# Attention, mixture of experts and gated layer in one kernel: attention steps in pairs, later weight splits, last k tile last

## The chip, the cores and the metric

The kernel runs on one core of a Trainium2 chip, in one launch. The metric is the device time of an execution in microseconds. PE is the matrix engine (TensorE), DVE the vector engine, ACT the scalar engine, POOL the GpSimd engine, SP the engine whose queue issues nearly all DMAs here. PE, DVE, ACT and POOL each work through their own instructions in program order, and they wait for one another through semaphores.

## The reference

For `q`, `k`, `v` of 2 x 8 x 576 x 64 two attentions are added. The coarse one averages four neighbouring positions of each and attends over the 144 that are left; the local one attends over the positions less than 4 away.

```python
q_d = q.reshape(B, H, Sd, factor, D).mean(axis=3)      # k_d and v_d likewise
out_d = sm_attn(q_d, k_d, v_d)
out_up = np.repeat(out_d, factor, axis=2)
mask = np.abs(pos[:, None] - pos[None, :]) < factor
...
return (out_up + out_local).astype(np.float32)
```

The result is `x`, 1152 tokens x 512. It goes through eight experts, `out += P[:, e] * (relu(x @ w1[e]) @ w2[e])` with 1024 hidden columns each, where `P` is a balanced gating of `x @ w_gate`. Then comes `(a * b) @ w_out` with `a = x @ w_a`, `b = x @ w_b`. All is float32.

## The kernel before, in words

**Precision.** A matrix is kept as a high part of type fp32r and the rest, a low part. A product is three matmuls: high by high, low by high, high by low. Splitting one weight block (128 x 512) is an ACT cast (L134) and a DVE subtraction (L135). A block lies in a ring of 13 slots, and three more lie in spare space. A weight load brings 256 KB into one of two staging buffers (tile `raw`, L409), and each buffer holds two blocks.

**Stages.** The experts are worked in units of half an expert. Tokens come in three blocks of 384 (`b` in the loop at L1297). In blocks 0 and 1 only the first two units (`n`, both halves of expert 0) are worked, while the attention of the later tokens is still running. For each unit there are four groups (`g_plain`, L446: 128 hidden columns by 384 tokens, four k tiles of 128, three matmuls each), whose result is a high and a low part of the hidden values. After the eight groups come six output tiles (`o_moe`, L488: 128 tokens by 512, twelve matmuls). After every group and every output tile `step()` (L1282) is called. In block 2 the same begins, the attention is over, the softmax of the gating runs beside it, and from there on products are combined in a way that saves one in eight. That part is some 85% of the time and isn't touched.

**Attention.** It is a generator, `side()` (L1103). There are 24 items (a third of a batch entry's positions, two heads), worked in a software pipeline of 29 iterations `s`. Each iteration is cut by `yield` into two half steps. The first half has, on PE, the transposes of q and k (a1) and the scores of the item before (b1); around them ACT copies and scales (a2, c3, d3), DVE maxima, sums and reductions (b4, b2, a3), and POOL the softmax's product and the low part `xl` of the result (L964, L1030). The second half has the products with v (d1) and the transposes of the probabilities (c1) on PE, on ACT the factor of the coarse output (d2a, L1010) and the exponentials (b3), on DVE d2 and c2, and on POOL the sums of four values (`sum_vd`, L865 and L868). Head pair 3, which fills k tile 3, comes last. When 384 tokens are complete, two more half steps make their gating logits (`logits`, L1039). In all 64 half steps do work, and the 65th call closes the attention (`close_attention`, L1231), which frees its buffers.

In a3 (L906), for the items that start a head pair (`u == 0`, eight of the 24), DVE sums four keys (L909) and multiplies the 128 x 144 result by 1/16 (L912, tile `kd`). The scores of the coarse attention (L931) use it one half step later.

**Order of the work.** It is fixed when the program is written. Before block 0 the loop at L1298 runs 23 half steps with nothing else; after each, `warm(3)` puts three dummy matmuls (tile `wz`, L1169; 16 stand at the very start) on PE, and after half steps 14, 16, 18, 20 and 22 one weight block is split. Then `step()` after a group splits one more block and adds 1.25 to a counter that pays for half steps, so that most groups are followed by one half step and each fourth by two. Ahead of the output tiles of block 0 the loop at L1315 splits what is missing of the 16 blocks. Before block 1 a half step is run if the tokens aren't complete (one is), and before block 2 what is left of the attention runs bare (six calls). `load_some` (L220) issues at most one weight load in each half step, and takes a staging buffer again two half steps after its second split.

**PSUM.** Groups and output tiles take turns in two banks (`bank("g")`), the attention in six.

Of the kernel before, what the change touches and what calls it, by code (L numbers as in the profile page):

```python
# [19 lines left out]
def attn_moe_glu_kernel(  # L20
# [16 lines left out]
    nc = tc.nc  # L37
# [6 lines left out]
    KT = DM // 128  # L44
    NT = N // 128
    NB = 3
    TB = N // NB
# [11 lines left out]
    def mm(o, l, r, start, stop, check=True):  # L59
        nc.tensor.matmul(out=o, lhsT=l, rhs=r, start=start, stop=stop, skip_group_check=not check)  # L60
# [11 lines left out]
    def bank(kind):  # L72
        if ps3 is not None and kind == "g":
            pool, tag = ps3, "g3"
        else:
            pool, tag = ps1, "g1"
        return pool.tile([128, 512], F32, tag=tag, name=tag)
# [6 lines left out]
    xh = xp.tile([128, KT, N], F32R, name="xh")  # L84
    xl = xp.tile([128, KT, N], F32R, name="xl")
# [6 lines left out]
    M = Model()  # L92
# [319 lines left out]
    units = []  # L412
    for e in range(E):
        for hf in range(2):
            u = Unit()
# [7 lines left out]
    for g in range(GU):  # L423
        u = Unit()
# [18 lines left out]

    GP = [[gp.tile([128, 4, TB], F32R, tag=f"{x}{n}", name=f"{x}{n}") for n in range(2)] for x in ("gh", "gl")]

    def g_plain(u, n, b, f, mid):  # L446

        gh, gl = GP[0][n], GP[1][n]
        cols = slice(b * TB, (b + 1) * TB)
        ps = bank("g")[:, :TB]  # L450
        k = 0
        for kt in range(KT):
            w = u.w[f // 2, kt // 2]
            o = (kt % 2) * 256 + (f % 2) * 128
            a_h, a_l = w.hi[:, o:o + 128], w.lo[:, o:o + 128]
            for l, r in ((a_h, xh), (a_h, xl), (a_l, xh)):
                mm(ps, l, r[:, kt, cols], k == 0, k == 3 * KT - 1)
                k += 1
        M.pe += 2.08
        for j in range(2):  # L460
            u.w[f // 2, j].use()
        if closed:
            pump(0.0)
        mid()
        nc.scalar.activation(out=gh[:, f], in_=ps, func=AF.Relu)
        nc.vector.scalar_tensor_tensor(
            out=gl[:, f], in0=ps, scalar=0.0, in1=gh[:, f].bitcast(F32),
            op0=ALU.max, op1=ALU.subtract,
        )
        act(0.5)  # L470
        dve(0.56)
# [434 lines left out]
    def a3(i, b, u, hp):  # L906
        if u == 0:
            kd_ = at.tile([128, SD], F32, tag=f"kd{hp}", name=f"kd{hp}", bufs=1)
            nc.vector.tensor_reduce(  # L909
                out=kd_, in_=kT[b, hp].rearrange("p (t r) -> p t r", r=4), axis=AX.X, op=ALU.add  # L910
            )
            nc.vector.tensor_scalar_mul(out=kd_, in0=kd_, scalar1=1.0 / 16.0)  # L912
            kd[b, hp] = kd_
        nc.vector.tensor_reduce(
            out=qdbd[i % 2].rearrange("p c h t -> p (c h t)"),
            in_=qbd[i % 2].rearrange("p c h (t r) -> p (c h t) r", r=4), axis=AX.X, op=ALU.add,
        )

    R = NC * 32

# [182 lines left out]
    def side():  # L1103
        n = len(order)
        done_l = 0

        def do(st, j):
            if 0 <= j < n:
                st(j, *order[j])

        for s in range(n + 5):
            if s == 5:
                wg32 = load_gate()
            if s == 9:
                gate_weights(wg32)
            if s + 2 < n:
                load_q(*order[s + 2])
                if order[s + 2][1] == 0:
                    load_k(order[s + 2][0], order[s + 2][2])
            if s < n:  # L1120
                load_v(*order[s])
                if order[s][:2] == (0, 0):
                    load_vd(0, order[s][2])
            do(a1, s)
            do(b1, s - 1)
            do(c3, s - 3)
            do(a2, s)
            do(b4, s - 2)
            do(d3, s - 4)
            do(b2, s - 1)  # L1130
            do(a3, s)
            yield
            do(d1, s - 3)
            do(d2a, s - 3)
            do(b3, s - 1)
            do(c1, s - 2)
            do(d2, s - 3)
            do(c2, s - 2)
            if 0 <= s - 2 < n and order[s - 2][1] == 0:
                sum_vd(order[s - 2][0], order[s - 2][2])  # L1140
            if 0 <= s - 1 < n and order[s - 1][:2] == (1, 0):
                load_vd(1, order[s - 1][2])
            yield
            while done_l <= ready[0]:
                yield from logits(done_l)
                done_l += 1
                yield
# [10 lines left out]
        )  # L1158


    WARM = (16, 3)
    SIDE = 1.25

    def warm(n):

# [5 lines left out]
    with tc.manual_schedule():  # L1171
# [53 lines left out]
        def run_first(n):  # L1225
            while n and wq:
                if len(units[1].o) == 4 and (wq[0].slot or not wq[0].ok()):
                    return
                n -= run(wq).slot
# [32 lines left out]
        def side_step():  # L1262
            if not closed:
                nsteps[0] += 1
                load_some()
            if gens[0] is None:
                return
            try:
                next(gens[0])
            except StopIteration:  # L1270
                if closed:
                    gens[0] = None
                else:
                    close_attention()
# [3 lines left out]
        tmp_stack = ExitStack()  # L1278
        turn = 0.0
        nside = 0  # L1280

        def step():  # L1282
            nonlocal turn
            if not closed:
                run_first(1)
                turn += SIDE
                while turn >= 1:
                    turn -= 1
                    side_step()
            else:  # L1290
                pump()

# [4 lines left out]
        for b in range(NB):  # L1297
            while ready[0] < b:  # L1298
                side_step()
                if b == 0:  # L1300
                    warm(WARM[1])
                nside += 1
                if nside > 12 and nside % 2 == 0:
                    run_first(1)
            if b == NB - 1:
                while not closed:
                    side_step()
                M.dve = M.act = M.pe
            for n in range(2):
                while len(units[n].w) < 4:  # L1310
                    run_first(1)
                for f in range(4):
                    g_plain(units[n], n, b, f, mid)
                    step()
            while len(units[1].o) < 4:  # L1315
                run_first(1)
            per = TB // 128
            firsts = [[
                lambda n=n, t=t, b=b: o_moe(
                    units[n], *([G[n][:, f] for f in range(4)] for G in GP), t, b * per + t, mid)  # L1320
                for t in range(per)
            ] for n in range(2)]
            for n in range(2 if b < NB - 1 else 1):
                for t in firsts[n]:
                    t()
                    step()
# [131 lines left out]
```

## Time and profile before

| what | us |
|---|---|
| median of 3 runs (lowest, highest) | 1088.69 (1088.54, 1089.17) |
| the profiled execution, its own time | 1087.57 |
| its span, first to last instruction | 1085.8 |
| first dummy matmul to the first group of block 0 | 1.32 to 47.23 |
| eight groups, six output tiles of block 0 | to 80.73, to 108.51 |
| eight groups, six output tiles of block 1 | to 139.55, to 163.47 |
| rest of the attention, alone | to 167.64 |

The times of the stages are read from the first PE instruction of each in the timeline. Busy times of PE are modelled at their ends, so that a PE shown busy may still be waiting for part of a fraction of a microsecond. An idle time stands in brackets behind an instruction, with the instruction that ended it.

### The profile page before, as it was taken

What the parts mean: (1) busy time and instruction counts of PE and PEld (TensorE: products, weight loads), DVE (VectorE), ACT (ScalarE), POOL (GpSimd) and SP (SyncE); (2) the same over time, 40 slices, a digit from 0 to 9 for tenths busy, and PEclk for the clock granted to TensorE, in tenths of its full rate; (3) what the DMA queues carried; (4) which work ended last, traced back from release to release, by engine and by line L of the source; (5) the groups of instructions that cost most, each with busy time, mean ns of one, the idle gap of its engine ahead of it and who ended that gap; (6) DMA issues with size and microseconds to landing.
All of it is one profiled execution on the core that took longest, in us unless ns stands there. A gap on an engine that the chain in (4) does not pass through costs nothing.

```text
span 1085.8 us, 18014 instructions
## 1 busy us (share of the span) xinstructions
PE 1073.7 (99%) x6569; PEld 974.8 (90%) x6569; DVE 788.2 (73%) x1545; ACT 456.8 (42%) x1135; POOL 516.0 (48%) x512
## 2 busy tenths in 40 slices
PE   9999999999999999999999999999999999999998
PEld 8898988899898999989899998989899899999997
DVE  7876546857888778888778788777854576677764
ACT  6664423454434453443444434444443553233221
POOL 3324116463645556464555645455561365355521
PEclk9999999999999999999999999999999999999999
DMA  7453100312323132422313232231311101111002
GB/s 172 126 143 88 23 5 6 102 59 86 98 89 103 64 124 66 130 94 84 112 54 125 76 130 96 71 118 48 124 61 45 45 1 59 59 46 53 20 21 88
DMA packets 80745, 84.52 MB, mean 78 GB/s; under 512 B 35856, under 2 KB 54288, under 8 KB 80656
## 3 DMA queue, kind: packets, MB, share of 16 engines
q1 hardware_dynamic: 79472, 83.07, 24.8%
q8 instruction: 52, 0.85, 0.3%
q10 hardware_dynamic: 1184, 0.30, 0.1%
q14 instruction: 37, 0.30, 0.1%
HBM read 71.54 MB, written 11.80 MB: 77 GB/s over the span
## 4 chain that ended last, share of the span: by engine, by line
PE 72%; DVE 0%; POOL 0%; ACT 0%; issue 0%; DVEq 0%
PE g L60 72%; PE g L787 0%; POOL gl L648 0%; DVE w L135 0%; DVE acc L1356 0%; DVE acc L513 0%; ACT G L644 0%; ACT gh L646 0%; DVE G L652 0%; DVEq L135 0%
## 5 line engine op out<-in xcount | busy, mean ns | idle before, releaser
L60 PE MATMUL g<-w,gh 128*128 128x512 f32 x1314 | 412.1, 395 | 0.3 <-DVE acc L513 0.3
L60 PE MATMUL g<-xh,w 128*128 128x256 f32 (+2 forms) x1536 | 339.1, 302 | 0.3 <-DVE lg L1053 0.3
L648 POOL TENSOR_TENSOR gl<-G,gh 128x256 fp32r<-128x256 f32 (+1 forms) x208 | 172.6, 839 | 264.8 <-ACT gh L646 253.4
L60 PEld LDWEIGHTS g<-w,gh 128*128 128x128 f32 x1314 | 235.8, 188 | 40.7 <-DVE acc L513 0.5
L60 PEld LDWEIGHTS g<-xh,w 128*128 128x128 f32 x1536 | 257.5, 189 | 4.6 <-DVE lg L1053 0.4
L60 PE MATMUL g<-w,gl 128*128 128x512 f32 x657 | 257.7, 392 | 0.0
L60 PE MATMUL g<-xl,w 128*128 128x320 f32 (+2 forms) x768 | 231.2, 301 | 1.4 <-POOL xl L1030 1.4
L135 DVE TENSOR_TENSOR w<-raw,w 128x512 fp32r<-128x512 f32 x139 | 137.2, 996 | 112.2 <-ACT w L134 112.1
L60 PE MATMUL g<-Th,w 128*128 128x320 f32 (+1 forms) x912 | 199.3, 295 | 0.0
L652 DVE TENSOR_TENSOR G<-g,G 128x256 f32<-128x256 f32 (+1 forms) x380 | 155.0, 449 | 21.4 <-PE g L60 10.1
L644 ACT ACTIVATE G<-G 128x256 f32<-128x256 f32 (+1 forms) x168 | 74.4, 443 | 212.8 <-DVE G L652 212.8
L60 PEld LDWEIGHTS g<-Th,w 128*128 128x128 f32 x912 | 152.2, 188 | 4.0 <-DVE G L652 1.0
L60 PEld LDWEIGHTS g<-xl,w 128*128 128x128 f32 x768 | 145.3, 189 | 6.2 <-POOL xl L1030 2.1
L60 PEld LDWEIGHTS g<-w,gl 128*128 128x128 f32 x657 | 123.4, 188 | 28.5
L60 PE MATMUL g<-Tl,w 128*128 128x256 f32 (+1 forms) x456 | 134.0, 294 | 0.0
L513 DVE SCALAR_TENSOR_TENSOR acc<-g,P,acc 128x512 f32<-128x512 f32 x126 | 93.8, 744 | 52.2 <-PE g L60 46.0
L646 ACT CAST gh<-G 128x256 fp32r<-128x256 f32 (+1 forms) x208 | 90.3, 434 | 92.1 <-DVE G L662 78.6
L134 ACT CAST w<-raw 128x512 fp32r<-128x512 f32 x180 | 107.6, 619 | 50.7 <-POOL raw L259 44.0
L389 POOL TENSOR_TENSOR dec<-dec 128x384 f32<-128x384 f32 x48 | 48.7, 1015 | 105.6 <-DVE dec L386 105.6
L60 PEld LDWEIGHTS g<-Tl,w 128*128 128x128 f32 x456 | 85.8, 188 | 3.1
L964 POOL TENSOR_TENSOR p<-p,rr 128x210 f32<-128x210 f32 x24 | 13.2, 551 | 107.1 <-DVE rr L963 29.9
L259 POOL TENSOR_TENSOR s<-raw 128x512 f32<-128x512 f32 x38 | 61.7, 1625 | 4.4 <-DMA raw<-w 3.8
(177 smaller groups left out, 1198.2 us busy)
## 6 DMA issues: line engine op xcount, KB each, us to landing
raw<-in_moe_w_dram SPq DMA_DIRECT2D x128, 256.0 KB
w<-dec SPq DMA_DIRECT2D x48, 192.0 KB
dec<-in_moe_w_a_dram SPq DMA_DIRECT2D x16, 384.0 KB
dec<-in_moe_w_b_dram SPq DMA_DIRECT2D x16, 384.0 KB
dec<-in_moe_w_out_dram SPq DMA_DIRECT2D x16, 384.0 KB
raw<-w SPq DMA_DIRECT2D x48, 128.0 KB
raw<-w SPq DMA_DIRECT2D x12, 256.0 KB
vw<-in_v_dram SPq DMA_DIRECT2D x72, 35.0 KB
```

Source lines behind the costliest of these rows:

```text
L60: nc.tensor.matmul(out=o, lhsT=l, rhs=r, start=start, stop=stop, skip_group_check=not check)
L134: nc.scalar.copy(out=hi, in_=raw)
L135: (low or nc.vector).tensor_tensor(out=lo, in0=raw, in1=hi.bitcast(F32), op=ALU.subtract)
L259: nc.gpsimd.tensor_tensor(out=o(), in0=A(*a), in1=A(*b), op=op)
L389: nc.gpsimd.tensor_tensor(out=tf, in0=tf, in1=mf, op=ALU.add)
L513: nc.vector.scalar_tensor_tensor(out=a, in0=ps, scalar=P[:, tt, u.e:u.e + 1], in1=a, op0=ALU.mult, op1=ALU.add)
L644: nc.scalar.activation(out=src, in_=src, func=AF.Relu)
L646: nc.scalar.copy(out=h, in_=src)
L648: nc.gpsimd.tensor_tensor(out=l, in0=src, in1=h.bitcast(F32), op=ALU.subtract)
L652: nc.vector.tensor_tensor(out=o, in0=bank_, in1=b, op=ALU.add)
L964: nc.gpsimd.tensor_tensor(out=p, in0=p, in1=rr[:, 0:NC].unsqueeze(2).to_broadcast([128, NC, W]), op=ALU.mult)
```

## The change

- `WARM` goes from (16, 3) to (16, 2): two dummy matmuls after each of the 23 half steps ahead of block 0.
- The multiplication by 1/16 moves from a3 on DVE to a new piece a4, an ACT multiplication in the second half step, behind d2a and ahead of b3.
- `SIDE` goes from 1.25 to 1.5, and half steps are run two at a time, when the counter has reached two.
- Only two weight blocks are split ahead of block 0 (after half steps 18 and 20). The other 14 are split by `step()` after the first eleven groups and tiles, by the list `share`. The loops that complete a unit's blocks ask for two ahead of its first group, for four ahead of its third, and for the output blocks of each unit ahead of that unit's tiles.
- In blocks 0 and 1 the first two groups of unit 0 are opened with k tiles 0 to 2, and each gets k tile 3 afterwards. Within a k tile the low part of the tokens comes last.

```diff
--- before.py
+++ after.py
@@ -443,20 +443,29 @@
 
     GP = [[gp.tile([128, 4, TB], F32R, tag=f"{x}{n}", name=f"{x}{n}") for n in range(2)] for x in ("gh", "gl")]
 
-    def g_plain(u, n, b, f, mid):
-
-        gh, gl = GP[0][n], GP[1][n]
+    def g_part(u, ps, b, f, kts):
+
         cols = slice(b * TB, (b + 1) * TB)
-        ps = bank("g")[:, :TB]
-        k = 0
-        for kt in range(KT):
+        for kt in kts:
             w = u.w[f // 2, kt // 2]
             o = (kt % 2) * 256 + (f % 2) * 128
             a_h, a_l = w.hi[:, o:o + 128], w.lo[:, o:o + 128]
-            for l, r in ((a_h, xh), (a_h, xl), (a_l, xh)):
-                mm(ps, l, r[:, kt, cols], k == 0, k == 3 * KT - 1)
-                k += 1
-        M.pe += 2.08
+            parts = (a_h, xh), (a_l, xh), (a_h, xl)
+            for k, (l, r) in enumerate(parts):
+                mm(ps, l, r[:, kt, cols], kt == 0 and k == 0, kt == KT - 1 and k == 2)
+        M.pe += 0.52 * len(kts)
+
+    def g_open(u, b, f):
+        ps = bank("g")[:, :TB]
+        g_part(u, ps, b, f, range(KT - 1))
+        return ps
+
+    def g_plain(u, n, b, f, mid, ps=None):
+
+        gh, gl = GP[0][n], GP[1][n]
+        if ps is None:
+            ps = g_open(u, b, f)
+        g_part(u, ps, b, f, (KT - 1,))
         for j in range(2):
             u.w[f // 2, j].use()
         if closed:
@@ -909,12 +918,15 @@
             nc.vector.tensor_reduce(
                 out=kd_, in_=kT[b, hp].rearrange("p (t r) -> p t r", r=4), axis=AX.X, op=ALU.add
             )
-            nc.vector.tensor_scalar_mul(out=kd_, in0=kd_, scalar1=1.0 / 16.0)
             kd[b, hp] = kd_
         nc.vector.tensor_reduce(
             out=qdbd[i % 2].rearrange("p c h t -> p (c h t)"),
             in_=qbd[i % 2].rearrange("p c h (t r) -> p (c h t) r", r=4), axis=AX.X, op=ALU.add,
         )
+
+    def a4(i, b, u, hp):
+        if u == 0:
+            nc.scalar.mul(out=kd[b, hp], in_=kd[b, hp], mul=1.0 / 16.0)
 
     R = NC * 32
 
@@ -1132,6 +1144,7 @@
             yield
             do(d1, s - 3)
             do(d2a, s - 3)
+            do(a4, s)
             do(b3, s - 1)
             do(c1, s - 2)
             do(d2, s - 3)
@@ -1158,8 +1171,8 @@
         )
 
 
-    WARM = (16, 3)
-    SIDE = 1.25
+    WARM = (16, 2)
+    SIDE = 1.5
 
     def warm(n):
 
@@ -1278,15 +1291,17 @@
         tmp_stack = ExitStack()
         turn = 0.0
         nside = 0
+        share = [1, 1, 1, 1, 1, 1, 2, 2, 1, 2, 1]
 
         def step():
             nonlocal turn
             if not closed:
-                run_first(1)
+                run_first(share.pop(0) if share else 1)
                 turn += SIDE
-                while turn >= 1:
-                    turn -= 1
-                    side_step()
+                if turn >= 2:
+                    for _ in range(2):
+                        turn -= 1
+                        side_step()
             else:
                 pump()
 
@@ -1300,20 +1315,23 @@
                 if b == 0:
                     warm(WARM[1])
                 nside += 1
-                if nside > 12 and nside % 2 == 0:
+                if nside in (18, 20):
                     run_first(1)
             if b == NB - 1:
                 while not closed:
                     side_step()
                 M.dve = M.act = M.pe
             for n in range(2):
-                while len(units[n].w) < 4:
+                while len(units[n].w) < 2:
                     run_first(1)
+                begun = {}
+                if n == 0 and not closed:
+                    begun = {f: g_open(units[n], b, f) for f in range(2)}
                 for f in range(4):
-                    g_plain(units[n], n, b, f, mid)
+                    while len(units[n].w) < 4 and f > 1:
+                        run_first(1)
+                    g_plain(units[n], n, b, f, mid, begun.get(f))
                     step()
-            while len(units[1].o) < 4:
-                run_first(1)
             per = TB // 128
             firsts = [[
                 lambda n=n, t=t, b=b: o_moe(
@@ -1321,6 +1339,8 @@
                 for t in range(per)
             ] for n in range(2)]
             for n in range(2 if b < NB - 1 else 1):
+                while len(units[n].o) < 4:
+                    run_first(1)
                 for t in firsts[n]:
                     t()
                     step()
```

## Rows read from the trace of the kernel before

**Rows 1.** The page: span, busy time of each engine, and slices of the span.
```profile
span 1085.8 us, 18014 instructions
...
PE 1073.7 (99%) x6569; PEld 974.8 (90%) x6569; DVE 788.2 (73%) x1545; ACT 456.8 (42%) x1135; POOL 516.0 (48%) x512
...
PE   9999999999999999999999999999999999999998
...
DVE  7876546857888778888778788777854576677764
...
PEclk9999999999999999999999999999999999999999
```

**Rows 2.** Windows: length, busy time (instructions) per engine, PEclk, DMA share, GB/s.
```profile
16.78:25.12 8.34, 8.04 (x74) 7.33 (x71) 7.74 (x23) 5.71 (x23) 4.21 (x6) 1.00 0.81 185
25.12:33.53 8.41, 7.65 (x66) 6.83 (x65) 7.98 (x23) 5.82 (x23) 4.19 (x6) 1.00 0.54 121
33.53:42.47 8.94, 8.10 (x72) 7.27 (x71) 7.77 (x24) 6.56 (x26) 5.02 (x8) 1.00 0.49 132
...
163.47:167.64 4.17, 2.52 (x14) 1.59 (x12) 0.94 (x4) 1.07 (x3) 2.21 (x3) 1.00 0.00 0
...
300.00:1085.00 785.00, 782.06 (x4679) 710.13 (x4678) 576.80 (x1022) 309.59 (x708) 392.40 (x366) 1.00 0.23 76
```

**Rows 3.** Timeline of PE, 0 to 48 us: start, duration, what, idle before.
```profile
1.32 3.57 PE L60 MATMUL g<-wz,identb 128*128 128x256 bf16 x16 [1.32 <-DVE wz L1176]
...
16.78 0.26 PE L60 MATMUL at<-mask,identb 128*128 128x210 bf16 x1
...
26.12 0.49 PE L60 MATMUL g<-wz,identb 128*128 128x256 bf16 x3
26.45 0.58 PE L60 MATMUL at<-pdT,vd 72*128 72x96 f32 x4
...
32.38 0.36 PE L975 MATMUL at<-ident,pd 96*72 96x96 f32 x2 [0.40 <-DVE pd L967]
...
39.72 0.69 PE L60 MATMUL at<-pdT,vd 72*128 72x96 f32 x4 [0.76 <-POOL vd L868]
...
47.23 0.42 PE L60 MATMUL g<-xh,w 128*128 128x384 f32 x1
```

**Rows 4.** Tile wz: all dummy matmuls, durations min/median/max.
```profile
L60 PE MATMUL g<-wz,identb x85: 270/273/421, 1.3 to 47.2; 128*128 128x256 bf16 x85
```

**Rows 5.** Timeline of DVE, 12 to 30 us, the coarse key factor.
```profile
12.49 0.52 DVE L912 TENSOR_SCALAR kd<-kd 128x144 f32<-128x144 f32 x1
...
19.33 1.27 DVE L912 TENSOR_SCALAR kd<-kd 128x144 f32<-128x144 f32 x1
...
27.71 1.29 DVE L912 TENSOR_SCALAR kd<-kd 128x144 f32<-128x144 f32 x1
```

**Rows 6.** Timeline of POOL, 18.5 to 31 us, one coarse value sum.
```profile
19.23 1.27 POOL L865 TENSOR_TENSOR rv<-rv 72x512 f32<-72x512 f32 x1
```

**Rows 7.** Tile kd: the coarse key factor over the whole run.
```profile
L912 DVE TENSOR_SCALAR kd<-kd x8: 234/806/1291, 7.4 to 83.6; 128x144 f32<-128x144 f32 x8
```

**Rows 8.** Timeline of ACT, 18 to 32 us, the operation ahead of the new factor.
```profile
23.67 0.25 ACT L1010 ACTIVATE od<-at 128x96 f32<-128x96 f32 x1 [1.59 <-PE at L60]
```

**Rows 9.** Timeline of PE, 50 to 118 us: three waits.
```profile
50.33 0.44 PE L60 MATMUL g<-xl,w 128*128 128x384 f32 x1 [1.09 <-POOL xl L1030]
...
110.88 0.45 PE L60 MATMUL g<-xl,w 128*128 128x384 f32 x1 [0.35 <-POOL xl L1030]
...
117.16 0.35 PE L1052 MATMUL at<-ident,lt 16*128 16x16 f32 x3 [0.56 <-ACT lt L1047]
```

**Rows 10.** Tile raw, 0 to 130 us: the two operations of a weight split.
```profile
L134 ACT CAST w<-raw x13: 609/611/625, 28.9 to 77.8; 128x512 fp32r<-128x512 f32 x13
...
L135 DVE TENSOR_TENSOR w<-raw,w x13: 674/692/694, 30.5 to 79.5; 128x512 fp32r<-128x512 f32 x13
```

**Rows 11.** The page's groups: the split's subtraction over the whole span.
```profile
L135 DVE TENSOR_TENSOR w<-raw,w 128x512 fp32r<-128x512 f32 x139 | 137.2, 996 | 112.2 <-ACT w L134 112.1
```

## The prediction

> **What bounds the kernel now.** I read the page first. PE is busy 99% of the span at full granted clock, DVE 73%, and only the first slices and the last show a PE digit that could hide much else [rows 1]. In the long part after 300 us PE is idle 2.9 of 785 us [rows 2]; nothing there is touched by the edits, and PE paces it, so microseconds won earlier should arrive at the end one for one. All the change can win lies ahead of 168 us.
>
> Second, the windows of the front, cut at the first matmul of a step's scores, so that each holds two iterations of the attention [rows 2]. From 16.78 to 33.53 us two iterations take 8.34 and 8.41 us. DVE is busy 7.74 and 7.98 of that, PE 8.04 and 7.65, and PE's share holds dummies. So the front has two engines that are almost full, DVE and PE, and it matters that the change relieves both.
>
> Third, the timelines of that stretch. On DVE one instruction stands out: the multiplication of the coarse keys takes 0.52, 1.27 and 1.29 us [rows 5], although its shortest takes 0.234 [rows 7]. The 1.27 us one starts 0.1 us after a POOL sum of 1.27 us and ends 0.1 us after it [rows 5, 6]: it stands still beside POOL's work. On PE the waits for DVE and POOL follow, such as 0.40 us for a late softmax product and 0.76 us for a coarse value sum [rows 3].
>
> Fourth, the waits after the front. PE waits 1.09 and 0.35 us for the low part of the last head pair in the first group of blocks 0 and 1, and 0.56 us for the logits of block 1 [rows 9]. When the attention's rest runs alone, PE is busy 2.52 of 4.17 us [rows 2].
>
> **The change part by part.**
>
> *Dummies.* Three of them hold PE for 0.33 us, from 26.12 to the next work at 26.45 [rows 3], so one costs 0.11 us. Of the 85 [rows 4], 16 stand at the start and 69 are 23 times three; 23 go: 2.5 us of PE. That is won where PE sets the pace, and is nothing where the next instruction waits for DVE or POOL anyway. Two iterations lose four dummies, 0.44 us.
>
> *Coarse key factor.* DVE loses 1.27 us in each of the two windows above. ACT gains an instruction that the trace doesn't show. Nearest is the scaling just ahead of it, 128 x 96 in 0.25 us [rows 8]; I take 0.3, between 0.2 and 0.6. ACT had waited 1.59 us for PE ahead of that scaling [rows 8] and is busy 5.7 to 6.6 us of an iteration pair [rows 2], so this hides. The new instruction waits for DVE's key sum, and behind it on ACT are the exponentials; but DVE's sum comes straight after the maxima which these need, and ACT arrives later still because of PE. I cost it at nothing; without that cover it would be about 0.7 us in each of four iterations, 2.8 us.
>
> *Splits moved out of the front.* Three blocks fewer: 3 x 0.69 us of DVE and 3 x 0.61 us of ACT [rows 10], all after 28 us.
>
> *Sum for the front.* It lasts from 1.32 to 47.23 us [rows 3]. For two iterations PE needs 7.65 - 0.44 = 7.2 us (the window with the most waits, so the one nearest to pure work), DVE 7.98 - 1.27 = 6.7 us [rows 2]. Two queues this full still make each other wait a little: I take 7.4 us, against 8.38 now, with 7.2 and 8.0 as bounds. The two windows give 2.0 us. The next, 8.94 us [rows 2], has a split of the three, a 0.76 us wait and four dummies; with the rest up to 47.23 I take 1.6 us (0.44 per two iterations for dummies is 0.7, half of the waits 0.9). From 9.8 to 16.78, 0.8 us (four dummies, and half a microsecond of DVE of which PE gets most). Before that, 0.3 us of the 0.5 us that its dummies cost, an estimate, because the pipeline is still filling there. Together 4.7 us, bounds 2.5 and 6.5.
>
> *Last k tile last.* The two opened groups put 18 matmuls ahead of the first use of k tile 3 and its low part is used last of all. By the kernel's own plan twelve of them are 2.08 us (L459), so that is over 3 us of work against a wait of 1.09 us. The first two waits of [rows 9] go, 1.44 us. No bank is short: the third group opens after the first has been read out.
>
> *Pairs at 1.5.* I counted half steps along the loops. Block 0's fourteen steps run 20 of them (numbers 24 to 43), so the single one ahead of block 1 is gone, and the logits' second half no longer follows their first at once: 0.56 us [rows 9]. Block 1's fourteen run 22 (44 to 65), and the 65th is the call that closes. So nothing is left to run bare: of 4.17 us, the 1.65 us in which PE idles go [rows 2], while its matmuls stay and move in between tiles. A pair puts two half steps' work on DVE behind one group, but there is a group or tile between any result and its use, as now.
>
> *Splits in the groups.* Fourteen in place of eleven there, each 0.61 us of ACT then 0.69 us of DVE [rows 10]. They hide behind a pair and a group, several microseconds of PE. Where two are split at once, DVE lags by about a microsecond and has the next tile to catch up. Weight loads of the second half of unit 0's blocks release the buffers later than now, so the first load of unit 1 starts only after the first group; I find a group and a pair between it and its split. First cost when this cover fails: a rival below.
>
> *A rule against it.* The 13 subtractions of splits by DVE take 0.69 us, none over 0.694, in the attention part [rows 10], yet 0.996 us on average over the span [rows 11]. The Trainium skill (GPSIMD Engine Reference, Key points) says that POOL shares SBUF interfaces with DVE instructions that have two SBUF inputs, which these have. By that rule 14 splits at 0.996 would take 4.3 us more of DVE than I reckon.
>
> *Sum.* The waits that go after the front: 1.44 + 0.56 + 1.65 = 3.65 us. PE's ends overlap the next start (three dummies are shown as 0.49 us but hand over after 0.33 [rows 3]), so each of the seven or so waits is 0.16 us longer than shown: 4.8 us. For new small waits of the denser mix I take off 0.6. That is 4.2, and with the front 8.9 us. The profiled execution took 1087.57 us (1.8 us outside its span): 1078.7. The median is 1.1 us above that execution, so 1079.8, say 1080.
>
> **The rivals.**
>
> 1. *The front gives little.* ACT and DVE hand work to each other within an iteration, and the time of a removed dummy or a stalled multiplication turns into a wait for the next result. For it: DVE and PE both had waits in the windows although both were full. Against: DVE shows no idle time before the stalled instructions [rows 5], so it passes on what it gains. The front gives 1.5 us: 1083.
>
> 2. *The bare end stays in part*, if the close falls one step later than I count or the last logits still wait for the last tokens: 1.65 + 0.5 us less, 1082.
>
> 3. *Splits just ahead of use become PE's waits* (the slower one). Place: PE's first matmul with a fresh block, in the second half of unit 0 and in unit 1's first group of block 0; the block's load could start only when the buffer was released one or two groups before. Uncovered, each costs 0.61 + 0.69 = 1.3 us, 14 of them 18.2 us: 1098. Seven uncovered cancel the gain; more than nine are slower by over 0.2%. For it: loads are now requested later. Against: of the 13 splits [rows 10], eight lie between groups now, and none of the waits of [rows 9] is theirs.
>
> 4. *The clock falls in the front.* The first 16 dummies took 3.57 us, 0.22 us each, about the 1.2 GHz pitch; later one takes 0.11, the 2.4 GHz pitch [rows 3]. Every microsecond of work at half clock adds one, so the gain is gone after 9 us of work, and the front with its some 33 us of work would end near 1113. Against: PE's busy share rises or stays when waits go together with dummies, and the granted clock is full throughout [rows 2]. The Trainium skill (TensorE: Matmul & The Clock Gate, Part 4: PE-mode transpose) says that transposes do not count as busy in the same way, and they are a good part of this front. No row here shows a clock that fell because of them.
>
> **How the numbers follow.** Forecast 1080: 62%. Rival 1: 16%. Rival 2: 6%. Rival 3: 8%, half of it slower and half of it near no change. Rival 4: 4%, mostly slower. Something else in between: 4%. About 0.2%, 2.2 us, is what a measurement of this kernel can tell from no change. Faster by more (forecast, rivals 1 and 2, most of the rest): 0.87; within: 0.06; slower: 0.07. The low end is the front at its bound of 6.5 us and no new waits, 8.9 + 1.8 + 0.6 = 11.3 us or 1077.4, and a little more if every dummy counts: 1076.5. The high end takes in rivals 1 and 2 and both together with some new waits: 1085.
>
> **What would show it.** Right: the first group starts near 42.5 us, with two iterations in about 7.4; no multiplication on DVE's coarse keys; PE's waits for `xl` gone; no stretch of attention alone ahead of block 2; granted clock full. Wrong: PE waits for ACT or DVE on tile `w`, SP or ACT waiting on `raw` loads in block 0; two iterations still over 8 us; a clock of half anywhere after the start; or more idle PE after 300 us.

## Result and profile after

The changed kernel takes 1079.15 us (median of five runs, 1078.53 to 1079.53), the kernel before 1088.69 us in the same job. The ratio is 0.9912, with a 95% interval of 0.9898 to 0.9927. The forecast was 1080.0 us in a range of 1076.5 to 1085.0.

The page of the changed kernel, its span and the busy time of its engines, against [rows 1]:

```profile
span 1077.4 us, 17982 instructions
...
PE 1069.1 (99%) x6546; PEld 972.7 (90%) x6546; DVE 783.1 (73%) x1537; ACT 458.1 (43%) x1143; POOL 517.3 (48%) x512
```

The span is 8.4 us shorter, and PE has 23 matmuls fewer (6569 to 6546), the dummies. The windows of the changed kernel (length, then busy time and instructions of PE, PEld, DVE, ACT, POOL, then granted clock, DMA share, GB/s), cut at the same places of the program as [rows 2]:

```profile
16.44:23.88 7.44, 7.35 (x67) 6.81 (x66) 6.72 (x22) 5.86 (x24) 4.21 (x6) 1.00 0.76 191
23.88:30.57 6.69, 6.69 (x60) 6.31 (x60) 6.03 (x20) 5.12 (x21) 4.20 (x6) 1.00 0.60 145
30.57:38.92 8.35, 7.70 (x68) 6.89 (x67) 7.60 (x24) 6.26 (x26) 5.04 (x8) 1.00 0.44 98
...
137.63:158.99 21.36, 21.36 (x111) 17.91 (x109) 7.43 (x18) 3.84 (x14) 7.57 (x10) 1.00 0.00 1
...
300.00:1077.00 777.00, 773.56 (x4627) 702.37 (x4625) 570.11 (x1007) 305.85 (x698) 388.86 (x361) 1.00 0.23 75
```

Two iterations of the attention fell from 8.34 and 8.41 us to 7.44 and 6.69, the third pair only from 8.94 to 8.35. The fourth row holds the six tiles of block 1 with the attention's end among them: PE is never idle, and nothing runs alone any more. After 300 us PE is as busy as before.

The timeline of PE in the changed kernel: its waits between 12 and 113 us, the first group of block 0, and the second half of block 1's logits:

```profile
35.67 0.69 PE L60 MATMUL at<-pdT,vd 72*128 72x96 f32 x4 [0.46 <-POOL vd L877]
...
37.24 0.39 PE L987 MATMUL at<-ident,pd 96*72 96x96 f32 x2 [0.19 <-DVE pd L979]
...
43.45 0.60 PE L60 MATMUL g<-xh,w 128*128 128x384 f32 x2
...
66.71 0.25 PE L60 MATMUL at<-mask,identb 128*128 128x210 bf16 x1 [0.27 <-ACT pd L965]
...
72.90 0.25 PE L60 MATMUL at<-mask,identb 128*128 128x210 bf16 x1 [0.66 <-ACT pd L965]
...
110.56 0.36 PE L1064 MATMUL at<-ident,lt 16*128 16x16 f32 x3
```

The front ends at 43.45 us, 3.78 us earlier than at 47.23 [rows 3]. The waits of [rows 9] are gone; the last of them, 0.56 us ahead of the logits, stood at 117.16 where 110.56 stands now. Two others are there instead, at 66.71 and 72.90: PE waits until ACT has read an older score out of its bank. The kernel before had one of this kind, 0.22 us at 79.83. From the first group of block 0 to the first of block 2 it was 120.41 us (47.23 to 167.64) and is 115.54 (43.45 to 158.99), 4.87 less; the rest takes 0.25 us more. 3.78 + 4.87 - 0.25 is the 8.4 us between the spans.

The tile `kd` of the changed kernel, against [rows 7]:

```profile
L929 ACT ACTIVATE kd<-kd x8: 315/322/324, 7.4 to 77.8; 128x144 f32<-128x144 f32 x8
```

The subtractions of its weight splits, against [rows 10], and four rows of them in the timeline of DVE:

```profile
L135 DVE TENSOR_TENSOR w<-raw,w x13: 676/693/1231, 34.9 to 82.4; 128x512 fp32r<-128x512 f32 x13
...
  DMA raw<-in_moe_w_dram: 0.6, 1
```

```profile
34.93 1.23 DVE L135 TENSOR_TENSOR w<-raw,w 128x512 fp32r<-128x512 f32 x1 [0.30 <-ACT w L134]
...
58.27 1.17 DVE L135 TENSOR_TENSOR w<-raw,w 128x512 fp32r<-128x512 f32 x1
...
71.02 1.68 DVE L135 TENSOR_TENSOR w<-raw,w 128x512 fp32r<-128x512 f32 x2
...
82.36 1.18 DVE L135 TENSOR_TENSOR w<-raw,w 128x512 fp32r<-128x512 f32 x1
```

The factor takes 0.32 us each on ACT, always. The median of the subtractions is that of before, 0.69 us, but three single ones took 1.17 to 1.23, and a pair 1.68 where another pair took 1.29. All four times a sum on POOL was under way when the subtraction started, the first time this one:

```profile
34.89 0.72 POOL L877 TENSOR_TENSOR vd<-rv 72x256 f32<-72x256 f32 x1
```

Once, for 0.6 us, a split waited for its load.

The median gained 9.5 us and the profiled execution 8.4. Of the 17 timed runs of the kernel before in one job, those with a mean granted clock of 0.999 or 1.0 (seven) have a median of 1087.3 us and those with 0.997 or 0.998 (ten) one of 1088.9; all five of the changed kernel have 0.999 or 1.0. The experiments on pairs show where this probably comes from.

### The profile page after: what moved, and what is told of

Its sections match the earlier page's. It is cut to its first block, busy times and chain, and to the rows that moved or that the text cites. A ratio compares the mean times of both kernels' runs of the same rounds, so it can differ in the third digit from the quotient of the medians.

```text
span 1077.4 us, 17982 instructions
## 1 busy us (share of the span) xinstructions
PE 1069.1 (99%) x6546; PEld 972.7 (90%) x6546; DVE 783.1 (73%) x1537; ACT 458.1 (43%) x1143; POOL 517.3 (48%) x512
## 5 line engine op out<-in xcount | busy, mean ns | idle before, releaser
L60 PE MATMUL g<-xh,w 128*128 128x256 f32 (+2 forms) x1536 | 334.9, 302 | 0.0
L135 POOL TENSOR_TENSOR w<-raw,w 128x512 fp32r<-128x512 f32 x41 | 54.7, 1341 | 23.1 <-ACT w L134 23.1
```

Source lines behind the costliest of these rows:

```text
L135: (low or nc.vector).tensor_tensor(out=lo, in0=raw, in1=hi.bitcast(F32), op=ALU.subtract)
```

## Experiments

All were timed in five rounds beside the kernel before. Unless said otherwise, differences are against the changed kernel's 1079.15 us. They were taken in three later jobs, in which the kernel before, at a mean clock of 0.999 or 1.0, had medians of 1087.6, 1087.4 and 1087.3 us. The part behind 200 us, which no edit touches, also differs from trace to trace, by up to some 0.5 us. So a difference of a few tenths of a microsecond isn't told from none.

### Three dummies again

```diff
-    WARM = (16, 2)
+    WARM = (16, 3)
```

> The changed kernel (1079.15 us) with three dummies after each half step instead of two, so 23 more of 0.11 us. Theory (with DVE relieved, PE sets the pace of most of the front): 1.5 to 2.5 us more, 1080.7 to 1081.7, first group of block 0 at about 45.5 instead of 43.45. Rival (the front is paced by DVE and ACT, a dummy only fills a wait): at most 0.8 us more, first group before 44.3.

Measured: 1079.38 us (1079.20 to 1080.05), 0.23 us more. The first group in its timeline of PE:

```profile
43.54 0.60 PE L60 MATMUL g<-xh,w 128*128 128x384 f32 x2
```

The first group starts 0.09 us later, although the 23 dummies take 2.5 us on PE: they cost next to nothing. The rival holds: the front is not paced by PE, and a dummy fills a wait. My sum for the front counted most of these 2.5 us.

### Coarse key factor back on DVE

```diff
-    nc.scalar.mul(out=kd[b, hp], in_=kd[b, hp], mul=1.0 / 16.0)
...
+    nc.vector.tensor_scalar_mul(out=kd_, in0=kd_, scalar1=1.0 / 16.0)
```

> The changed kernel with the coarse key factor back on DVE, right behind the key sum. Theory (the multiplication stands still beside POOL's coarse value sum, and PE has little slack left to hide it): at least two of the first four take over 1 us again, and 1.5 to 3 us more, 1080.7 to 1082. Rival (with the front's other parts moved it no longer meets the POOL sum, and 0.23 us each hides): under 0.5 us more, 1079 to 1079.6.

Measured: 1080.85 us (1080.44 to 1080.89), 1.70 us more, first group at 45.77, 2.3 us later. Two rows of its timeline of DVE:

```profile
19.30 1.24 DVE L921 TENSOR_SCALAR kd<-kd 128x144 f32<-128x144 f32 x1
...
27.66 1.32 DVE L921 TENSOR_SCALAR kd<-kd 128x144 f32<-128x144 f32 x1
```

and of POOL:

```profile
19.18 1.27 POOL L874 TENSOR_TENSOR rv<-rv 72x512 f32<-72x512 f32 x1
...
27.61 1.27 POOL L874 TENSOR_TENSOR rv<-rv 72x512 f32<-72x512 f32 x1
```

Each multiplication ends 0.1 us behind the POOL sum that was under way when it started (20.54 against 20.45, 28.98 against 28.88). The theory holds. The Trainium skill (SBUF — State Buffer, SBUF: two separate sides) says that DVE operations that use two ports and GpSimd operations take a shared pair of ports exclusively and for a whole instruction. The trace agrees: the multiplication lasts until POOL's instruction is over, 1.0 and 1.1 us longer than the undisturbed 0.235.

### Splits early again

```diff
-                if nside in (18, 20):
+                if nside > 12 and nside % 2 == 0:
...
-        share = [1, 1, 1, 1, 1, 1, 2, 2, 1, 2, 1]
+        share = []
```

> The changed kernel with five blocks split ahead of block 0 as before (after half steps 14 to 22) and one after each group, the missing three ahead of the tiles of unit 1. Theory (three subtractions and casts more in a front without slack): 0.5 to 2 us more, 1079.7 to 1081. Rival (after its relief DVE has room for them, and the waits of 0.27 and 0.66 us in block 0 that come behind casts on ACT go away): 0.5 to 1 us less, 1078.2 to 1078.7.

Measured: 1080.10 us (1079.82 to 1080.59), 0.95 us more. Two rows of its timeline of PE:

```profile
37.47 0.69 PE L60 MATMUL at<-pdT,vd 72*128 72x96 f32 x4 [0.97 <-POOL vd L877]
...
44.76 0.59 PE L60 MATMUL g<-xh,w 128*128 128x384 f32 x2
```

The front is 1.3 us longer, as the theory has it. But some 0.5 us of that isn't the splits' own work: it is in the wait of 0.97 us, which was 0.46 in the changed kernel. What PE waits for there is the POOL sum of this row, and a split on DVE started at 36.14 us, just ahead of it:

```profile
36.18 1.24 POOL L877 TENSOR_TENSOR vd<-rv 72x256 f32<-72x256 f32 x1
```

The same sum took 0.72 us in the changed kernel, where it started 0.04 us ahead of the split, and there the split was the longer one. The kernel before had this collision too, ahead of its wait of 0.76 us [rows 3]:

```profile
38.39 0.69 DVE L135 TENSOR_TENSOR w<-raw,w 128x512 fp32r<-128x512 f32 x1 [0.24 <-ACT w L134]
```

```profile
38.43 1.24 POOL L868 TENSOR_TENSOR vd<-rv 72x256 f32<-72x256 f32 x1
```

So of a split and a sum that meet, the later one stands still, and where that is the sum, PE waits longer for it.

### Single half steps at 1.25

```diff
-    SIDE = 1.5
+    SIDE = 1.25
...
-                if turn >= 2:
-                    for _ in range(2):
-                        turn -= 1
-                        side_step()
+                while turn >= 1:
+                    turn -= 1
+                    side_step()
```

> The changed kernel with half steps paid at 1.25 and run one at a time, as before. Theory (the rest of the attention runs bare again ahead of block 2, and block 1's logits follow each other at once): 2.2 to 3.2 us more, 1081.4 to 1082.4, with 3 to 4 us of attention alone ahead of block 2. Rival (pairs cost as much in waits behind ACT as they save there): under 1 us more.

Measured: 1083.40 us (1082.23 to 1083.55), 4.25 us more, beyond the theory's range. The windows of this run, the end of the attention alone and the 3.4 us from 162.3:

```profile
156.70:161.90 5.20, 3.59 (x22) 2.63 (x20) 1.61 (x4) 1.07 (x3) 2.17 (x3) 1.00 0.00 0
162.30:165.70 3.40, 3.40 (x13) 3.40 (x12) 0.84 (x2) 0.00 (x0) 3.20 (x5) 0.50 0.00 0
```

Right behind the bare stretch, in which PE was busy 3.59 of 5.20 us, the granted clock is half, 1.2 GHz. That costs what is at half: 3.4 us hold work of 1.7. The one of the five runs with a mean clock of 1.0 took 1082.23 us, 3.1 more, which is inside the range; the four with 0.998 took 1083.25 to 1083.55.

### Single half steps, the bare end filled with dummies

```diff
                 while not closed:
                     side_step()
+                    if not closed:
+                        warm(WARM[1])
```

on top of the edit above.

> As u4_single_steps (1083.4 us), with two dummies after each half step that runs alone ahead of block 2, some ten of 0.11 us. Theory (some 1.7 us of what single steps cost are a fall of the clock to 1.2 GHz for 3.4 us after that stretch, in which PE idles; busier, it keeps the clock): 0.5 to 1.7 us less than u4_single_steps, 1081.7 to 1082.9, full clock there. Rival (the fall has nothing to do with PE's idling, or the time was lost to the waits alone): the same or up to 1 us more.

Measured: 1082.48 us (1082.12 to 1082.89), 0.92 us less than single half steps alone, although ten dummies were added. Its windows:

```profile
157.00:162.30 5.30, 4.42 (x31) 3.38 (x30) 1.76 (x5) 1.07 (x3) 2.35 (x3) 1.00 0.00 0
162.40:165.80 3.40, 3.40 (x23) 3.40 (x21) 1.41 (x3) 0.49 (x1) 3.34 (x5) 1.00 0.00 0
```

With PE busier ahead, 4.42 of 5.30 us, the clock stays full, in all five runs (0.999 or 1.0). So the bare end had two prices: its waits, and in most runs the clock behind it. The kernel before has the same bare end, with PE busy 2.52 of 4.17 us [rows 2]; its profiled execution kept the clock in the window behind it, which is why the trace could not show me the second price:

```profile
167.70:171.00 3.30, 3.30 (x19) 3.30 (x20) 1.53 (x3) 0.49 (x1) 3.24 (x5) 1.00 0.00 0
```

### Groups not opened

```diff
-                if n == 0 and not closed:
+                if False:
```

> The changed kernel without opened groups: each of the first two groups runs its four k tiles at once, with the low part of the tokens still last within a k tile. Theory (the low part of head pair 3 comes about 0.8 us later than the group wants it in block 0, and in time in block 1, which pairs have moved away): 0.4 to 1.3 us more, 1079.5 to 1080.4, one wait of PE for xl. Rival (the order within the k tile is enough): no difference, no such wait.

Measured: 1079.54 us (1079.36 to 1079.62), 0.39 us more, just under the theory's range. The only wait for the low part in its timeline of PE:

```profile
45.76 0.44 PE L60 MATMUL g<-xl,w 128*128 128x384 f32 x1 [0.34 <-POOL xl L1042]
```

The wait is there, but 0.34 us instead of 1.09 [rows 9]. The opening takes off only this; the rest had gone without it, by the low part coming last or by DVE and POOL running less late. Which of the two it was wasn't tried.

### One dummy, and none

```diff
-    WARM = (16, 2)
+    WARM = (16, 1)
```

> The changed kernel with one dummy after each half step. Theory (PE sets the pace): 1.5 to 2.5 us less, 1076.7 to 1077.7. Rival 1 (DVE and ACT set it): at most 0.7 us less, waits of PE for them instead. Rival 2 (the clock): some stretch of the front at 1.2 GHz and several us more.

and with `(16, 0)`:

> The changed kernel with no dummies but the 16 at the start. Theory (PE sets the pace until the dummies are used up, then DVE, whose work of two iterations is some 6.7 to 7 us): 2 to 4 us less, 1075 to 1077, the second step smaller than the first. Rival 1 (DVE and ACT set it already): under 1 us less. Rival 2 (the clock): matmuls at the pitch of 1.2 GHz in the front and up to 30 us more.

Measured: 1078.56 us with one (1078.16 to 1080.66, four runs) and 1078.72 with none (1077.99 to 1085.90, six runs). The runs with a mean clock of 0.999 or 1.0, three of four and four of six, lie at 1078.16 to 1078.81 and 1077.99 to 1078.78. So 23 more dummies taken away are worth some 0.8 us there, and the last 23 nothing. In the other three the clock fell, among them both profiled executions. With one dummy, two windows, the wait in the first, and the POOL sum that PE waits for:

```profile
33.70:37.50 3.80, 2.62 (x25) 2.32 (x23) 3.41 (x11) 2.39 (x9) 3.64 (x6) 1.00 0.56 127
37.60:41.00 3.40, 3.40 (x21) 3.29 (x19) 2.60 (x9) 3.31 (x13) 0.07 (x2) 0.51 0.64 146
```

```profile
36.17 0.69 PE L60 MATMUL at<-pdT,vd 72*128 72x96 f32 x4 [1.19 <-POOL vd L877]
```

```profile
34.89 1.23 POOL L877 TENSOR_TENSOR vd<-rv 72x256 f32<-72x256 f32 x1
```

and with none:

```profile
31.80:38.00 6.20, 4.75 (x41) 4.12 (x39) 5.56 (x18) 5.17 (x20) 3.91 (x6) 1.00 0.54 122
38.00:51.70 13.70, 13.70 (x66) 13.50 (x66) 8.62 (x26) 6.28 (x24) 3.30 (x7) 0.50 0.31 74
```

Both rivals are seen, one in time and one in risk. The pace of the front is not PE's: without dummies PE is busy only 4.75 of 6.20 us. The first two windows of two iterations took 7.42 and 6.46 us with none, 7.44 and 6.57 with one, 7.44 and 6.69 with two, 7.61 and 6.94 with three, though each step is four dummies, 0.44 us on PE. And behind such idling the clock can fall, here for 13.7 us, which made that profiled execution's span 1084.1 us. In both profiled executions the longest wait ahead of the fall, 1.19 and 1.41 us, was that of the matmul that reads this POOL sum (the profile of the second puts it down to DVE, but the sum ended as late, 0.05 us ahead of the matmul). A split had held the sum up: it took 1.23 us in both, as in the row above. Two dummies kept the clock in all five runs of the changed kernel, at a cost under 1 us.

### The coarse key factor alone, in the kernel before

```diff
-            nc.vector.tensor_scalar_mul(out=kd_, in0=kd_, scalar1=1.0 / 16.0)
...
+            do(a4, s)
             do(b3, s - 1)
```

with `a4` as in the change, and nothing else of it.

> The kernel before with nothing but the coarse key factor moved to ACT. Theory (the front is paced by DVE, ACT and what they hand each other, and the multiplication that stands still beside POOL was its largest removable piece, 2.3 us when it was put back into the changed kernel): 1.7 to 3 us less than the kernel before, 1085.5 to 1086.8, first group near 45. Rival (three dummies and five splits would take its place): under 0.8 us less.

Measured: 1087.34 us (1085.12 to 1089.13, twelve runs) against 1088.77 before, a ratio of 0.9989 (0.9980 to 0.9997). That is 1.4 us less, between the two expectations. Its timeline of PE at the first group, and the window behind its bare end:

```profile
45.21 0.42 PE L60 MATMUL g<-xh,w 128*128 128x384 f32 x1
...
48.40 0.44 PE L60 MATMUL g<-xl,w 128*128 128x384 f32 x1 [0.94 <-POOL xl L1033]
```

```profile
166.60:170.00 3.40, 3.40 (x12) 3.40 (x11) 0.49 (x2) 0.30 (x1) 2.88 (x5) 0.50 0.00 0
```

The first group starts 2.0 us earlier than in the kernel before, with three dummies and five splits still in place, as the theory has it; behind the attention 1.7 us of that are left. The clock doesn't hide it: the three runs at full clock (1085.12 to 1086.20) have a median of 1085.8 against 1087.3 before, the nine with 0.998 one of 1087.4 against 1088.9, 1.5 us less at either. The wait for the low part is nearly as long as before.

### Split between the half steps of a pair

```diff
                 turn += SIDE
                 if turn >= 2:
-                    for _ in range(2):
-                        turn -= 1
-                        side_step()
+                    turn -= 2
+                    side_step()
+                    run_first(n)
+                    side_step()
+                else:
+                    run_first(n)
```

with `n = share.pop(0) if share else 1` ahead of it in place of the `run_first` there.

> The changed kernel with the weight split of a step put between the two half steps of its pair, so that its casts come behind the exponentials on ACT. Theory (the waits of 0.27 and 0.66 us for the exponentials in block 0, 1.26 us with the emptied pipeline, come from casts ahead of them): 0.8 to 1.3 us less, 1077.8 to 1078.4, those waits gone. Rival (they come from the coarse key factor on ACT or the late start of the pair): under 0.3 us of difference, waits still there; or the blocks come late and PE waits for them.

Measured: 1078.07 us (1077.64 to 1078.12), 1.08 us less. ACT in the changed kernel ahead of the wait at 72.90:

```profile
70.38 1.13 ACT L134 CAST w<-raw 128x512 fp32r<-128x512 f32 x2
...
71.55 0.32 ACT L929 ACTIVATE kd<-kd 128x144 f32<-128x144 f32 x1
...
72.37 0.39 ACT L965 ACTIVATE pd<-at,nd 96x144 f32<-96x144 f32 x1
```

and in this run, with the PE instruction that no longer waits:

```profile
71.31 0.31 ACT L929 ACTIVATE kd<-kd 128x144 f32<-128x144 f32 x1
...
72.13 0.38 ACT L965 ACTIVATE pd<-at,nd 96x144 f32<-96x144 f32 x1
...
72.48 1.14 ACT L134 CAST w<-raw 128x512 fp32r<-128x512 f32 x2
```

```profile
72.30 0.26 PE L60 MATMUL at<-mask,identb 128*128 128x210 bf16 x1
```

The two casts of 1.13 us had stood ahead of the exponentials that PE waits for. Behind them they cost nothing, and both waits are gone from the timeline. The coarse key factor still stands ahead, and no wait is left: it isn't the cause. The exponentials end only 0.25 us earlier, though, and PE starts 0.60 earlier, before the last of them is over; in the changed kernel it had waited for that one too. Why it no longer does isn't shown. These 0.60 us are all that the two traces differ by up to 700 us: the end of the first wait brings nothing (66.69 against 66.71). The other 0.45 of the 1.1 us between the spans arise later, in work that the edit doesn't touch.

### Splits between, and the two early ones later

```diff
-                if nside in (18, 20):
+                if nside in (20, 22):
```

on top of the edit above.

> The changed kernel with the split between the half steps of a pair (as in s1_split_between, 1078.07 us) and the two early splits after half steps 20 and 22 instead of 18 and 20. Theory (the split after half step 18 meets the POOL sum for head pair 3, stands at 1.23 us and makes the softmax product 0.19 us late): 0.2 to 0.8 us less than s1_split_between, 1077.3 to 1077.9, no wait for pd near 37 us. Rival (the POOL sum itself is what PE waits for, and a later split is late for the first group): no change or more.

Measured: 1077.70 us (1077.33 to 1078.00), a ratio to before of 0.9903 (0.9888 to 0.9917); 0.37 us less than the run above, whose range, 1077.64 to 1078.12, overlaps with this one. The first split in the timeline of DVE, at 34.93 and 1.23 us long in the changed kernel, is here:

```profile
39.11 0.69 DVE L135 TENSOR_TENSOR w<-raw,w 128x512 fp32r<-128x512 f32 x1 [0.30 <-ACT w L134]
```

In the changed kernel a POOL sum started at 34.89 us, just ahead of it, and here none does. The wait of 0.19 us for the softmax product is gone. What that is worth isn't shown: the profiled execution ends 0.05 us ahead of the run above, and in it PE waited 1.08 us at 23.82 for a load of k. This version's median is 1.45 us below the changed kernel's, and all its runs lie below all of that one's.

### The value sums half a step earlier as well

```diff
+            if 0 <= s - 2 < n and order[s - 2][1] == 0:
+                sum_vd(order[s - 2][0], order[s - 2][2])
             do(a1, s)
...
             do(c2, s - 2)
-            if 0 <= s - 2 < n and order[s - 2][1] == 0:
-                sum_vd(order[s - 2][0], order[s - 2][2])
```

on top of the edit above.

> As c1_between_later, and the coarse value sums on POOL half a step earlier, ahead of the softmax product, where POOL waits over 2 us. Theory (PE's wait of 0.46 us for the last sum goes): 0.3 to 0.8 us less than c1_between_later. Rival (the sums hold up the product behind them on POOL, or slow DVE's multiplications): the same or more.

Measured: 1081.08 us (1079.01 to 1084.26, six runs), 3.4 us more than without. The windows of its start:

```profile
9.20:12.40 3.20, 1.79 (x16) 1.30 (x13) 2.60 (x8) 2.01 (x9) 2.02 (x3) 1.00 0.70 152
12.40:22.60 10.20, 9.69 (x49) 9.13 (x50) 5.27 (x17) 5.26 (x20) 3.56 (x5) 0.50 0.80 214
```

Its timelines of POOL and of DVE in the first of these windows:

```profile
10.30 1.26 POOL L874 TENSOR_TENSOR rv<-rv 72x512 f32<-72x512 f32 x1 [7.66 <-DMA rv<-in_v_dram]
...
12.32 0.53 POOL L976 TENSOR_TENSOR p<-p,rr 128x210 f32<-128x210 f32 x1
```

```profile
10.68 0.97 DVE L979 TENSOR_SCALAR pd<-pd,rr 96x144 f32<-96x144 f32 x1
```

The rival holds, and in both ways: the first sum waits for its load until 10.30 us and makes the softmax product behind it late (12.32, and 10.31 without the edit), and DVE's multiplication, 0.29 us elsewhere, stands until POOL's sum ends at 11.56. PE is busy 1.79 of 3.20 us there, and the clock falls behind it. The two runs at full clock took 1079.01 and 1079.32 us, still 1.3 and 1.6 us more than without the edit.

## Why the prediction was right, step by step

**The time.** 1079.15 us against 1080.0. The sum was 8.9 us for the profiled execution; it gained 8.4. That it came so close is in part luck: the front gave 0.9 us less than forecast, the part behind it 4.87 us against 4.2, and the two misses nearly cancel. The median gained 1.1 us more than the execution, a distance that I had taken as fixed. Most likely it is the clock behind the bare end: the fall was traced there in two kernels with a bare end, 3.4 us at half, which is 0.0016 of the span and costs 1.7 us, and ten of 17 runs of the kernel before had a mean clock 0.002 to 0.003 lower and took 1.6 us longer. No trace of such a run of the kernel before was kept.

**Dummies: the term was mis-sized.** I put 2.5 us of PE there and counted most of it in the front's sum. Put back, they cost 0.23 us, and taking away as many again won some 0.8. My 7.2 us for two iterations was PE's busy time less its dummies, and 6.69 lies below it: what a window shows as busy on PE isn't all work. My first rival, that their time turns into a wait for the next result, is what the runs show.

**The coarse key factor: right, and larger.** It stood beside POOL's sum as the rows said, and it is the front's largest piece: 2.3 us at the first group when put back, 2.0 when it is the only edit. On ACT it takes 0.32 us (0.3 estimated), and PE has no wait for it.

**Splits out of the front: right, with a part that I had not seen.** 1.3 us at the first group, 0.95 in time. I counted only the work of three splits. The wait of 0.76 us that I read in [rows 3] was partly a split's doing: it held the POOL sum up for 0.5 us.

**The front's sum.** 4.7 us forecast, 3.78 measured, first group at 43.45 and not at 42.5. The three edits undone one at a time move the first group by 0.1, 2.3 and 1.3 us, together 3.7, so here they add up. By stretches, I forecast 1.1 us ahead of the first window, 2.0 in the first two and 1.6 behind them, and 0.34, 2.62 and 0.82 came. The forecast of 7.4 us for two iterations came out as 7.44 and 6.69, but 8.35 in the third pair, over the 8 us that I had named as a sign of being wrong. There I had most waits vanish; the wait for the last value sum stayed (0.46 of 0.76 us), and a stretched split came in. What sets the 7.4 us that remain without any dummies wasn't settled: DVE, ACT and POOL all have some idle time there. My reading that the page's first slices leave room on PE was wrong, they all read 9 [rows 1]; the windows were what showed the front.

**Last k tile last: mechanism right, credit wrong.** The waits went. The opening of groups accounts for 0.39 us at most, for a wait of 0.34; in block 1 no wait came back without it.

**Pairs: right, undersized.** The half steps fell as counted, the 65th call closed the attention at the end of block 1, and the logits' halves stand apart. I took 0.56 and 1.65 us of idle time and some 0.16 us for each wait. Single half steps cost 3.1 us at full clock and 4.25 in the median. That a stretch in which PE idles can also cost the clock behind it is what the term left out.

**New small waits.** 0.6 us was set aside. They are 0.27 and 0.66 us behind casts on ACT; without them the median is 1.08 us lower, of which the traces show 0.60 at that place. I had named the DVE lag of the double splits and not the ACT queue.

**The rule on two SBUF inputs.** Four of the 16 subtractions of the attention part met a POOL sum and took 0.4 to 0.5 us longer, some 1.9 us of DVE in all against the 4.3 that I had reckoned for 14; the median is 0.693 as before. So the rule from the prediction held where they met. Most of this fell on DVE behind the front, where PE shows no wait for DVE. It works the other way as well, on POOL, and that way PE waits.

**The rivals.** Splits never became waits for their blocks, except for 0.6 us of ACT on one load. The clock held in the changed kernel, transposes and all; that it can fall in this front is shown by three of the ten runs with fewer dummies, after stretches in which PE idled. Whether transposes count for it wasn't isolated.

The parts undone one at a time sum to 0.23 + 1.70 + 0.95 + 0.39 + 4.25 = 7.5 of 9.5 us, or at full clock, with 3.1 for the pairs, 6.4 of 8.1. The rest wasn't traced; it may lie with what wasn't undone, such as the order within a k tile, and with parts that cover for one another.

## What to carry to other kernels

When PE is shown 99% busy but some of its work is filler, look for the engine that paces the stretch by removing the filler: if nothing is won, the filler costs nothing and may be keeping the clock. An instruction with one duration in most places and five times that in others is worth lining up with the other engines' rows; moved to an engine that doesn't share what it waits for, it gave back its whole stall here. Of two instructions that shut each other out, see which one starts first and which one the bottleneck waits for: 0.04 us decided here whether a split or the sum that PE wanted stood still. In an in-order queue, put work that is needed late behind work whose result frees a bank.

## What was not expected of the hardware

The granted clock fell to half although PE had been busy for more than half of the time just before: 2.62 of 3.80 us with one dummy, 4.75 of 6.20 with none, 3.59 of 5.20 at the bare end. It was kept behind 2.52 of 4.17 in the kernel before. It came in some executions of one program and not in others (four of five with single half steps), so that one profiled execution, as that of the kernel before, can miss a cost that most executions pay.

A DVE subtraction and a POOL sum that meet stop one another in either direction: 1.23 and 0.72 us where the sum started first, 0.69 and 1.24 where the subtraction did.

At its very start the profile doesn't show the clock. The window of the first 16 dummies in the kernel before reads 1.00:

```profile
1.32:4.69 3.37, 3.37 (x17) 2.43 (x17) 1.73 (x14) 1.28 (x1) 1.06 (x5) 1.00 0.81 171
```

Yet they take 0.21 us each, 256 columns at 1.2 GHz, and a later one 0.11: here the pitch of the matmuls tells the level.
